# Another order for the opening of a one-core kernel: two loads on a second queue, zeroed decay rows, and an earlier read of the state sums

## The chip, the cores and the metric

The kernel runs on one core of one Trainium2 chip. The time is the device time of one execution, in microseconds; seven executions of the kernel before are given by their median. A profile of one execution gives the span (from the first to the last instruction of the program), every instruction with its engine and duration, and every DMA issue. The engines are TensorE (PE, with its weight loads PEld), VectorE (DVE), ScalarE (ACT), GpSimd (POOL) and SyncE (SP); SP and ACT also issue DMAs, and those entries are written SPq and ACTq.

## The reference

A recurrent attention with decay (batch 4, 8 heads, 768 tokens, head size 64), whose output is fed to a two-layer network with a leaky ReLU:

```python
gamma = 1.0 - 2.0 ** (-5.0 - np.arange(H))
for t in range(S):
    state = gamma[None, :, None, None] * state + einsum('bhd,bhe->bhde', k[:, :, t], v[:, :, t])
    y[:, :, t] = einsum('bhd,bhde->bhe', q[:, :, t], state) / sqrt(D)
x = y.transpose(0, 2, 1, 3).reshape(B * S, H * D)      # 3072 x 512
h = x @ w_in                                           # 512 x 2048
out = np.maximum(0.01 * h, h) @ w_out                  # 2048 x 512
```

The weights are float64 in memory; the rest is float32.

## The kernel before

The tokens are worked in six chunks of 128 (c = 0 to 5), each for four batches (b = 0 to 3). For one chunk and batch, `score` multiplies keys by queries into PSUM (L165), `masked` multiplies that by a triangular mask on VectorE into SBUF (L187), `decay_v` scales the values by a decay table (L147, or L151 on ScalarE), `reads` multiplies the state of earlier chunks by the queries (L201), `values` multiplies the masked scores by the values (L210), and `taken` scales the sum on VectorE and writes it to the token block x (L255). `state` sums keys times values (L225), and `state_taken` adds this to the state and decays it (L260, L261). For chunks 2 to 5 the score and the state sums have PSUM banks of their own (`score_apart`, L294, and `states_apart`), and `visit_with_scores` runs the attention of two batches between two stages of the network.

The network multiplies each block of 512 tokens by eight units of weights. A product of 2 x 2 blocks is made with seven block products instead of eight (`seven`, L521), from sums and differences of the blocks (L467, L470); `hidden` makes the first layer with the leaky ReLU (L556), `output` the second. Only the first unit of chunk 0 is multiplied plainly, in `direct` (tile d, L543): four steps for each half of the tokens, each step with one more piece of the weights, since the pieces come one after the other.

A piece of weights is 128 x 512 float64 words, loaded raw (L394) and made float32 in two parts. `powers` makes the powers of two out of the exponent bits with three ScalarE instructions (L440, L442, L443) and uses the piece's own float32 place as scratch. `mantissas` makes the rest on VectorE: the upper bits (L452), the lower bits added (L461), the product with the power (L463).

The order on each engine is the program's; nothing reorders it. The change lies in the opening, written out by hand at L688 to L790. All loads but one go through SP's queue in this order: queries and keys of batch 0, its values, those of batch 1, weight pieces 0 and 1, queries and keys of batch 2, its values, pieces 2 and 3, batch 3, the keys needed for the states, then chunk 1. ScalarE's queue carries one, eight rows of decay tables (L696), which land in a corner of the tile t and are spread to 128 partitions by three small products: the decay per head and the decay per chunk into `tables` (L742, L744), and the decay per token into `spread` (L748); copies bring these to the SBUF tile `dec` (L747 on VectorE, L750 on ScalarE).

`keep_busy(n)` (L730) issues n products of zeros, which keep TensorE at work while it has nothing to do: seven at the start, one between the values of batches 0 and 1, three after the score of batch 2. Their zeros are 128x256 words of t, set on VectorE (L725). The mask is set on VectorE (L713) and made triangular on POOL (L714).

The order on TensorE is then: seven idle products, score 0, tables, spread, score 1, values 0, one idle product, values 1, score 2, three idle products, and the first two steps of d. On VectorE: mask of score 0, the copy of the tables, the decay of values 0, mask of score 1, x of batch 0, upper bits of piece 0, x of batch 1, the rest of piece 0, piece 1, mask of score 2, piece 2. On ScalarE: the copy of `spread`, powers of pieces 0 and 1, decay of values 2, powers of pieces 2 and 3. On POOL: the decay of values 1.

Of the kernel before, what the change touches and what calls it, by code (L numbers as in the profile page):

```python
# [9 lines left out]
FP32 = mybir.dt.float32  # L10
U32 = mybir.dt.uint32
U16 = mybir.dt.uint16
I16 = mybir.dt.int16
BF16 = mybir.dt.bfloat16
I64 = mybir.dt.int64
AF = mybir.ActivationFunctionType
ALU = mybir.AluOpType
# [6 lines left out]
def kernel(  # L24
# [35 lines left out]
    nc = tc.nc  # L60
    NC = S // C
    DM = H * D
    HP = H // 2
    NU = DF // 512
    N = B * C // 2
    f64 = weights.dtype == I64
# [3 lines left out]
    work = ctx.enter_context(tc.tile_pool(name="work", bufs=1))  # L70
# [44 lines left out]
    heads = {}  # L115
# [11 lines left out]
            y = flat[:, half : 2 * half].rearrange("p (s h d) -> p s h d", s=2, h=H)  # L127
        heads[c, b] = x, y

    def load_qk(c, b):  # L130
        nc.sync.dma_start(out=heads[c, b][0], in_=qk[c, b])

    def load_v(c, b):
        nc.sync.dma_start(out=heads[c, b][1][:, 1], in_=kv[c, b][:, 1])

    def load_k(c, b):
        nc.sync.dma_start(out=heads[c, b][1][:, 0], in_=kv[c, b][:, 0])
# [6 lines left out]
    def decay_v(c, b, engine=nc.gpsimd):  # L144
        v = heads[c, b][1][:, 1]
        if engine is not nc.scalar:
            engine.tensor_tensor(out=v, in0=v, in1=gk.unsqueeze(2).to_broadcast([128, H, D]),  # L147
                                 op=ALU.mult)
        else:
            for h in range(H):  # L150
                engine.activation(v[:, h], v[:, h], AF.Identity, scale=gk[:, h : h + 1])  # L151
# [6 lines left out]
    def score(c, b):  # L158

        x = heads[c, b][0]  # L160
        ps = scores[c, b] = two_banks(f"ap_{c}_{b}")
        for a in range(HP):
            for u in range(2):
                for j in range(2):
                    nc.tensor.matmul(ps[ts(u, 64), j, a, :], lhsT=x[ts(j, 64), 1, a, ts(u, 64)],  # L165
                                     rhs=x[ts(j, 64), 0, a, :])
# [18 lines left out]
    def masked(c, b):  # L185
        am = new_am(c, b)
        nc.vector.tensor_tensor(  # L187
            out=am.rearrange("p j a t -> p (j a) t"),
            in0=scores[c, b].rearrange("p j a t -> p (j a) t"),
            in1=mask.unsqueeze(1).to_broadcast([128, H, C]), op=ALU.mult)  # L190
        scores[c, b] = am
# [54 lines left out]
    def taken(c, b, xb):  # L246

        tokens_taken(c, b, xb)
        state_taken(c, b, for_state(sums_at[c, b]))
# [5 lines left out]
        nc.vector.tensor_tensor(out=blocks, in0=ps[:, :, 0 : HP // 2, :], in1=gq, op=ALU.mult)  # L255

    def state_taken(c, b, sp):
        sums_at.pop((c, b))
        if 0 < c < NC - 1:
            nc.vector.tensor_tensor(out=st[b], in0=st[b], in1=sp, op=ALU.add)  # L260
            nc.vector.tensor_tensor(out=st[b], in0=st[b],  # L261
                                    in1=gc.unsqueeze(2).to_broadcast([128, HP, D]), op=ALU.mult)

# [65 lines left out]
    def visit_with_scores(c, b, following, complete=False):  # L329

        x = xs[c][0]
        early, late = ((following[0], following[1] + i) for i in range(2))
        score_apart(*early)
        for i in range(2):
            reads(c, b + i)
        masked_apart(*early, 0)
        masked_apart(*early, 1)
        score_apart(*late)  # L340
        for i in range(2):
            values(c, b + i)
        masked_apart(*late, 0)
        for i in range(2):
            tokens_taken(c, b + i, x)
        sp = states_apart(c, b)
        if complete:
            if xs[c][1] is None:
                xs[c][1] = new_t(c, f"t_{c}")
            t = xs[c][1]  # L350
            for k in range(2):
                minus(t[:, 0, k], x[:, 1, k], x[:, 0, k])
                minus(t[:, 1, k], x[:, 3, k], t[:, 0, k])
        masked_apart(*late, 1)
        if complete:
            minus(t[:, 2], x[:, 2], t[:, 1])
            last_difference(x)
        for i in range(2):
            state_taken(c, b + i, sp[:, i])
        for i in range(2):  # L360
            ahead(c + 1, b + i)
        for at in (early, late):
            load_kv(*at)
        for at in (early, late):
            decay_v(*at)
# [3 lines left out]
    raws = {}  # L369
# [5 lines left out]
    def piece(n):  # L375

        k, h, i = n // 4, n // 2 % 2, n % 2
        if k < N_UNITS - 1:
            return unit(k)[:, 2 * h : 2 * h + 2, i, :]
        new_pair(h)  # L380
        return units[k][h][:, :, i, :]
# [11 lines left out]
            raws[n] = place.bitcast(I64)  # L393
        nc.sync.dma_start(out=raws[n], in_=weights[n])  # L394

    def next_powers():
        n = done["powers"]
        done["powers"] += 1
        if n < N_PIECES and f64:
            powers(n)  # L400

    def next_mantissas(between=None):

        n = done["mantissas"]
        done["mantissas"] += 1
        if f64 and between is None:
            mantissas(n)
        elif f64:
            mantissas_upper(n)
            between()  # L410
            mantissas_rest(n)
        elif between is not None:
            between()
        if n != 3:
            load_piece(n + 4 if n < 3 else n + 3)
        if n == N_PIECES - 1:
            new_pair(2)
            for b in range(AHEAD):
                load(2, b)
        if n % 4 == 3 and n > 7:  # L420
            add_sums(n // 4)

    def round_piece():

        next_mantissas()
        next_powers()

    zs = {}

    def powers(n):  # L430

        top = raws[n].bitcast(U16).rearrange("p (h n four) -> p h n four", four=4, h=2)[:, :, :, 3]
        z = zs[n] = work.tile([128, 2, W // 2], I16, tag="z", bufs=3, name=f"z{n}")
        x = piece(n)


        nc.scalar.activation(x, top, AF.Prelu, alpha=float(BEND), scale=1.0 / 16,  # L440
                             bias=-7.5 / 16 - TOP)
        nc.scalar.activation(z, x, AF.Prelu, alpha=1.0 / BEND, bias=-float(BEND))  # L442
        nc.scalar.activation(z.bitcast(U16), z, AF.Relu, scale=128.0, bias=32768.0)  # L443

    def mantissas(n):

        mantissas_upper(n)
        mantissas_rest(n)

    def mantissas_upper(n):  # L450
        hi = raws[n].bitcast(U32).rearrange("p (h n two) -> p h n two", two=2, h=2)[:, :, :, 1]
        nc.vector.tensor_scalar(out=piece(n).bitcast(U32), in0=hi, scalar1=0x000FFFFF,  # L452
                                scalar2=0x00100000, op0=ALU.bitwise_and, op1=ALU.bitwise_or)

    def mantissas_rest(n):
        z = zs.pop(n)
        words = raws.pop(n).bitcast(U32).rearrange("p (h n two) -> p h n two", two=2, h=2)
        lo = words[:, :, :, 0]
        f = piece(n)
        m = f.bitcast(U32)  # L460
        nc.vector.scalar_tensor_tensor(out=f, in0=lo, scalar=2.0 ** -32, in1=m,  # L461
                                       op0=ALU.mult, op1=ALU.add)
        nc.vector.scalar_tensor_tensor(out=f, in0=f, scalar=2.0 ** -20, in1=z.bitcast(BF16),  # L463
                                       op0=ALU.mult, op1=ALU.mult)

    def plus(out, a, b):
        nc.vector.tensor_tensor(out=out, in0=a, in1=b, op=ALU.add)  # L467
# [1 line left out]
    def minus(out, a, b):  # L469
        nc.vector.tensor_tensor(out=out, in0=a, in1=b, op=ALU.subtract)  # L470
# [21 lines left out]
    def last_difference(x):  # L492
        minus(x[:, 1], x[:, 3], x[:, 1])
# [198 lines left out]
    words = tile_x("words").rearrange("p i k n -> p (i k n)")[:, 0 : 2 * W]  # L692
    xs = {0: new_x(0)}
    x, t = xs[0]
    rows = t[0:H, 1:3].rearrange("p i k n -> p (i k n)")[:, 0 : decay.shape[1]]
    nc.scalar.dma_start(out=rows, in_=decay)  # L696
    load_qk(0, 0)
    load_v(0, 0)
    load_qk(0, 1)
    load_v(0, 1)  # L700
    load_piece(0)
    load_piece(1)
    load_qk(0, 2)
# [17 lines left out]

    nothing = t[:, 0, 0, :].bitcast(BF16)
    nc.vector.memset(t[:, 0, 0, :], 0.0)  # L725
    idle = psum.tile([128, 2, N], FP32, tag="ff", bufs=4, name="idle")

    def keep_busy(n):
        for _ in range(n):
            nc.tensor.matmul(idle.rearrange("p i n -> p (i n)"), lhsT=nothing[:, 0:128],  # L730
                             rhs=nothing, start=True, stop=True, skip_group_check=True)

# [2 lines left out]
    n_gq = HP * C  # L737
    ends = [0, C, C + H, 2 * C + H, 2 * C + H + n_gq, 2 * C + H + n_gq + HP]
    by_head, ones, place, g_q, g_c = (rows[:, i:j] for i, j in zip(ends, ends[1:]))
    keep_busy(7)  # L740
    score(0, 0)
    nc.tensor.matmul(tables[:, 0, 0:H], lhsT=by_head, rhs=ones, start=True, stop=True,  # L742
                     skip_group_check=True)
    nc.tensor.matmul(tables[:, 0, H : H + HP], lhsT=place, rhs=g_c, start=False, stop=True,  # L744
                     skip_group_check=True)
    masked(0, 0)
    nc.vector.tensor_copy(out=dec[:, n_gq:], in_=tables[:, 0, 0 : H + HP])  # L747
    nc.tensor.matmul(spread.rearrange("p i n -> p (i n)"), lhsT=place, rhs=g_q, start=True,  # L748
                     stop=True, skip_group_check=True)
    nc.scalar.copy(out=dec[:, 0:n_gq], in_=spread.rearrange("p i n -> p (i n)"))  # L750
    decay_v(0, 0, nc.vector)
    score(0, 1)
    values(0, 0)
    masked(0, 1)
    decay_v(0, 1)
    keep_busy(1)
    next_powers()
    taken(0, 0, x)
    values(0, 1)
    next_mantissas(lambda: taken(0, 1, x))  # L760
    next_powers()
    score(0, 2)
    keep_busy(3)
    steps = direct(0, 0, x, parts[0][1], 0)
    next(steps)
    next_mantissas()
# [204 lines left out]
```

## Time and profile before

| | |
|---|---|
| median of seven executions | 666.54 us (665.59 to 669.92) |
| the profiled execution | 665.59 us |
| its span | 663.9 us, 10517 instructions |
| TensorE busy | 657.9 us (99%) |
| VectorE, ScalarE, POOL busy | 368.7, 176.1 and 18.9 us |
| read from and written to memory | 41.97 and 6.29 MB |

A line of the profile gives the kernel's line, the engine, the operation, the tiles (out<-in), and the partitions by elements. In the timeline a row begins with its start and its length in us from the span's start; "x16" counts the instructions put together in it, and the bracket tells how long the engine had been idle and what ended that. A matmul of float32 is counted as two instructions. In the chain of work that ended last, each piece follows what released it.

### The profile page before, as it was taken

How to read it: one execution, taken by the hardware profiler on the slowest of the kernel's cores; microseconds unless marked ns; L12 is line 12 of the kernel's file. 1: busy time of each engine (PE TensorE's matmuls, PEld its weight loads, DVE VectorE, ACT ScalarE, POOL GpSimd, SP SyncE). 2: the span in 40 equal slices, each digit the busy share in tenths (PEclk: the TensorE clock that was granted, in tenths of full speed). 3: DMA queues.
4: the chain of work that ended last, by engine and by line, in shares of the span. 5: the costliest groups of instructions: out<-in, count | busy, mean ns of one | idle time of the engine just before them, and what ended most of it. 6: DMA issues, size and time to landing. Idle time of an engine off the chain costs nothing.

```text
span 663.9 us, 10517 instructions
## 1 busy us (share of the span) xinstructions
PE 657.9 (99%) x4537; PEld 574.4 (87%) x4537; DVE 368.7 (56%) x588; ACT 176.1 (27%) x322; POOL 18.9 (3%) x22
## 2 busy tenths in 40 slices
PE   8999999999999999999999999999999999999998
PEld 5888888888888888888888889888888888888886
DVE  5789969889888674243436414527333343431342
ACT  5854555264261002202102211300220210221210
POOL 0000000000000020001001001001000100000000
PEclk9999999999999999999999999999999999999999
DMA  8920312312322550020022003004000001000001
GB/s 327 402 100 33 126 64 74 117 65 105 118 69 90 223 192 1 0 99 30 1 86 105 1 1 127 1 16 176 1 0 32 34 0 48 17 0 1 1 0 63
DMA packets 15757, 48.92 MB, mean 74 GB/s; under 512 B 1752, under 2 KB 2008, under 8 KB 15712
## 3 DMA queue, kind: packets, MB, share of 16 engines
q1 hardware_dynamic: 15696, 48.24, 20.1%
q8 instruction: 35, 0.57, 0.3%
q14 instruction: 10, 0.08, 0.0%
q10 hardware_dynamic: 16, 0.02, 0.0%
HBM read 41.97 MB, written 6.29 MB: 73 GB/s over the span
## 4 chain that ended last, share of the span: by engine, by line
PE 98%; DMA 1%; SPq 1%; issue 0%; DVE 0%
PE B_o L521 13%; PE A_o L521 13%; PE C_o L521 12%; PE A_h L521 12%; PE C_h L521 12%; PE B_h L521 12%; PE D_o L521 6%; PE D_h L521 6%; PE yp L210 3%; PE d L543 2%; PE ap L294 2%; PE ap L165 1%; PE yp L201 1%; DMA in<-in_qk_dram 1%; PE sp L225 1%; PE yp L225 0%
## 5 line engine op out<-in xcount | busy, mean ns | idle before, releaser
L521 PE MATMUL A_h<-x,w 128*128 128x256 f32 x368 | 87.7, 381 | 0.0
L521 PEld LDWEIGHTS A_h<-x,w 128*128 128x128 f32 x368 | 69.3, 190 | 9.7 <-issue 0.2
L521 PE MATMUL A_o<-g,w 128*128 128x256 f32 x288 | 68.1, 379 | 0.0
L467 DVE TENSOR_TENSOR m<-m,B_h 128x512 f32<-128x512 f32 x23 | 15.8, 686 | 92.8 <-PE B_h L521 92.8
L521 PEld LDWEIGHTS A_o<-g,w 128*128 128x128 f32 x288 | 54.6, 190 | 7.6 <-issue 0.2
L561 ACT COPY m<-A_h 128x512 f32<-128x512 f32 x23 | 13.5, 586 | 175.8 <-PE A_h L521 155.5
L556 ACT ACTIVATE g<-g 128x512 f32<-128x512 f32 x69 | 42.0, 630 | 66.0 <-DVE g L467 66.0
L467 DVE TENSOR_TENSOR m<-m,B_o 128x512 f32<-128x512 f32 x16 | 11.0, 685 | 64.3 <-PE B_o L521 64.3
L521 PE MATMUL D_h<-t,w 128*128 128x256 f32 x184 | 43.5, 379 | 0.0
L521 PE MATMUL C_h<-x,w 128*128 128x256 f32 x184 | 43.5, 379 | 0.0
L521 PE MATMUL B_h<-t,w 128*128 128x256 f32 x184 | 43.5, 379 | 0.0
L521 PE MATMUL C_h<-t,w 128*128 128x256 f32 x184 | 43.5, 379 | 0.0
L521 PE MATMUL B_h<-x,w 128*128 128x256 f32 x184 | 43.5, 379 | 0.0
L521 PEld LDWEIGHTS B_h<-t,w 128*128 128x128 f32 x184 | 35.0, 190 | 4.8
L521 PEld LDWEIGHTS D_h<-t,w 128*128 128x128 f32 x184 | 35.0, 190 | 4.8
L521 PEld LDWEIGHTS C_h<-x,w 128*128 128x128 f32 x184 | 35.0, 190 | 4.8
L521 PEld LDWEIGHTS C_h<-t,w 128*128 128x128 f32 x184 | 35.0, 190 | 4.8
L521 PEld LDWEIGHTS B_h<-x,w 128*128 128x128 f32 x184 | 35.0, 190 | 4.8
L470 DVE TENSOR_TENSOR gd<-g,gd 128x512 f32<-128x512 f32 x48 | 33.2, 692 | 1.7
L521 PE MATMUL B_o<-gd,w 128*128 128x256 f32 x144 | 34.0, 379 | 0.0
L521 PE MATMUL C_o<-gd,w 128*128 128x256 f32 x144 | 34.0, 379 | 0.0
L521 PE MATMUL D_o<-gd,w 128*128 128x256 f32 x144 | 34.0, 379 | 0.0
(125 smaller groups left out, 996.2 us busy)
## 6 DMA issues: line engine op xcount, KB each, us to landing
raw<-in_weights_dram SPq DMA_DIRECT2D x31, 512.0 KB, 4.0
kv<-in_kv_dram SPq DMA_DIRECT2D x17, 512.0 KB, 5.0
out_dram<-o SPq DMA_DIRECT2D x23, 256.0 KB, 2.3
qk<-in_qk_dram SPq DMA_DIRECT2D x11, 512.0 KB, 3.6
o<-in_qk_dram SPq DMA_DIRECT2D x8, 512.0 KB, 3.4
in<-in_qk_dram SPq DMA_DIRECT2D x5, 512.0 KB, 7.8
in<-in_kv_dram SPq DMA_DIRECT2D x3, 512.0 KB, 8.1
kv<-in_kv_dram SPq DMA_DIRECT2D x4, 256.0 KB, 6.8
```

Source lines behind the costliest of these rows:

```text
L165: nc.tensor.matmul(ps[ts(u, 64), j, a, :], lhsT=x[ts(j, 64), 1, a, ts(u, 64)], rhs=x[ts(j, 64), 0, a, :])
L201: nc.tensor.matmul(ps[ts(i, 64), j, m, :], lhsT=st[b][ts(j, 64), a, :], rhs=x[ts(j, 64), 0, a, :], start=(m == 0), stop=False, skip_group_ ...
L210: nc.tensor.matmul(ps[ts(i, 64), j, m, :], lhsT=y[:, 1, 2 * a + j, :], rhs=am[:, j, a, :], start=(c == 0 and m == 0), stop=True, skip_grou ...
L225: nc.tensor.matmul(sp[ts(j, 64), a, :], lhsT=y[:, 0, 2 * a + j, :], rhs=y[:, 1, 2 * a + j, :], start=start, stop=True, skip_group_check=True)
L294: nc.tensor.matmul(ps[j][ts(u, 64), a, :], lhsT=x[ts(j, 64), 1, a, ts(u, 64)], rhs=x[ts(j, 64), 0, a, :])
L467: nc.vector.tensor_tensor(out=out, in0=a, in1=b, op=ALU.add)
L470: nc.vector.tensor_tensor(out=out, in0=a, in1=b, op=ALU.subtract)
L521: nc.tensor.matmul(half, lhsT=block(w, sa)[:, k, ts(i, 128)], rhs=rhs[:, k, :], start=(first and (i == 0 or split) and n == 0 and k == 0), ...
L543: nc.tensor.matmul(banks[r][:, i, :], lhsT=block(2 * u, r + 2 * kh)[:, k, ts(i, 128)], rhs=x[:, 2 * kh + th, k, :], start=(step == 0 and i ...
L556: nc.scalar.activation(g[:, i], g[:, i], AF.Prelu, alpha=0.01)
L561: nc.scalar.copy(out=got["m1"], in_=ps)
```

## The change

Four things are done. First, batch 1's queries and keys are asked for on ScalarE's queue, ahead of everything else there, and its values on the same queue after the decay rows. Second, the decay rows lie on 128 partitions that were set to zero before (half by POOL, half by VectorE), so that the three small products run over 128 partitions instead of 8; their load waits for these zeros. Third, the order of the opening is another one: ten idle products at the start and one after the score of batch 2; both scores come before `spread`; the copy of `tables` is ScalarE's, and the decay of values 0 and of values 1 is POOL's; pieces 0 and 1 get scratch tiles for their powers; and the VectorE work on piece 0 is laid around the x of batches 0 and 1. Fourth, in `visit_with_scores` both additions of the state sums come before the last difference of x, and both decays after it.

```diff
-    def load_qk(c, b):
-        nc.sync.dma_start(out=heads[c, b][0], in_=qk[c, b])
+    def load_qk(c, b, queue=nc.sync):
+        queue.dma_start(out=heads[c, b][0], in_=qk[c, b])
...
     def state_taken(c, b, sp):
+        state_added(c, b, sp)
+        state_decayed(c, b)
...
@@ visit_with_scores
             minus(t[:, 2], x[:, 2], t[:, 1])
+        for i in range(2):
+            state_added(c, b + i, sp[:, i])
+        if complete:
             last_difference(x)
         for i in range(2):
-            state_taken(c, b + i, sp[:, i])
+            state_decayed(c, b + i)
...
-        x = piece(n)
+        x = piece(n) if scratch is None else scratch
...
@@ the opening
-    rows = t[0:H, 1:3].rearrange("p i k n -> p (i k n)")[:, 0 : decay.shape[1]]
-    nc.scalar.dma_start(out=rows, in_=decay)
+    rows = t[:, 1:3].rearrange("p i k n -> p (i k n)")[:, 0 : decay.shape[1]]
+    nothing = t[:, 0, 0, 0:64].bitcast(BF16)
+    half = decay.shape[1] // 2
     load_qk(0, 0)
+    load_qk(0, 1, nc.scalar)
+    nc.vector.memset(t[:, 0, 0, 0:64], 0.0)
+    nc.gpsimd.memset(rows[:, :half], 0.0)
+    nc.vector.memset(rows[:, half:], 0.0)
+    nc.scalar.dma_start(out=rows[0:H], in_=decay)
     load_v(0, 0)
-    load_qk(0, 1)
-    load_v(0, 1)
+    load_v(0, 1, nc.scalar)
     load_piece(0)
...
-    nothing = t[:, 0, 0, :].bitcast(BF16)
-    nc.vector.memset(t[:, 0, 0, :], 0.0)
...
-            nc.tensor.matmul(idle.rearrange("p i n -> p (i n)"), lhsT=nothing[:, 0:128],
-                             rhs=nothing, start=True, stop=True, skip_group_check=True)
+            nc.tensor.matmul(idle.rearrange("p i (two n) -> p (i two) n", two=2), lhsT=nothing,
+                             rhs=nothing.unsqueeze(1).to_broadcast([128, 4, 128]),
+                             start=True, stop=True, skip_group_check=True)
...
-    keep_busy(7)
+    keep_busy(10)
     score(0, 0)
...
     masked(0, 0)
-    nc.vector.tensor_copy(out=dec[:, n_gq:], in_=tables[:, 0, 0 : H + HP])
+    nc.scalar.copy(out=dec[:, n_gq:], in_=tables[:, 0, 0 : H + HP])
+    decay_v(0, 0)
+    score(0, 1)
+    decay_v(0, 1)
+    masked(0, 1)
     nc.tensor.matmul(spread.rearrange("p i n -> p (i n)"), lhsT=place, rhs=g_q, start=True,
                      stop=True, skip_group_check=True)
     nc.scalar.copy(out=dec[:, 0:n_gq], in_=spread.rearrange("p i n -> p (i n)"))
-    decay_v(0, 0, nc.vector)
-    score(0, 1)
     values(0, 0)
-    masked(0, 1)
-    decay_v(0, 1)
+    values(0, 1)
+    next_powers(scratch("m1", 0))
+    begin_mantissas(lambda: taken(0, 0, x))
+    taken(0, 1, x)
+    end_mantissas()
+    next_powers(scratch("u2", 1))
+    score(0, 2)
     keep_busy(1)
-    next_powers()
-    taken(0, 0, x)
-    values(0, 1)
-    next_mantissas(lambda: taken(0, 1, x))
-    next_powers()
-    score(0, 2)
-    keep_busy(3)
     steps = direct(0, 0, x, parts[0][1], 0)
```

`begin_mantissas` issues the upper bits, then what it is given, then the lower bits; `end_mantissas` the product with the power and the next load. Without an argument the two together are what `next_mantissas` was.

More of the change, by code (lines that the diff above doesn't have):

```diff
@@ L128, in place_for, with load_v @@
         heads[c, b] = x, y
-    def load_qk(c, b):
-        nc.sync.dma_start(out=heads[c, b][0], in_=qk[c, b])
-    def load_v(c, b):
-        nc.sync.dma_start(out=heads[c, b][1][:, 1], in_=kv[c, b][:, 1])
+    def load_qk(c, b, queue=nc.sync):
+        queue.dma_start(out=heads[c, b][0], in_=qk[c, b])
+    def load_v(c, b, queue=nc.sync):
+        queue.dma_start(out=heads[c, b][1][:, 1], in_=kv[c, b][:, 1])
     def load_k(c, b):
@@ L257, in state_taken, with state_added @@
     def state_taken(c, b, sp):
+        state_added(c, b, sp)
+        state_decayed(c, b)
+    def state_added(c, b, sp):
         sums_at.pop((c, b))
@@ L260, in state_taken, with state_decayed @@
             nc.vector.tensor_tensor(out=st[b], in0=st[b], in1=sp, op=ALU.add)
+    def state_decayed(c, b):
+        if 0 < c < NC - 1:
             nc.vector.tensor_tensor(out=st[b], in0=st[b],
@@ L394, in load_piece, with next_powers @@
         nc.sync.dma_start(out=raws[n], in_=weights[n])
-    def next_powers():
+    def next_powers(scratch=None):
         n = done["powers"]
@@ L399, in next_powers, with begin_mantissas, end_mantissas @@
         if n < N_PIECES and f64:
-            powers(n)
-    def next_mantissas(between=None):
+            powers(n, scratch)
+    def begin_mantissas(between=None):
+        mantissas_begun(done["mantissas"], between)
+    def end_mantissas():
         n = done["mantissas"]
         done["mantissas"] += 1
[L406 to L413, printed above, removed]
+        mantissas_ended(n)
         if n != 3:
@@ L421, in next_mantissas @@
             add_sums(n // 4)
+    def next_mantissas():
+        begin_mantissas()
+        end_mantissas()
     def round_piece():
@@ L428, with powers @@
     zs = {}
-    def powers(n):
+    def powers(n, scratch):
         top = raws[n].bitcast(U16).rearrange("p (h n four) -> p h n four", four=4, h=2)[:, :, :, 3]
         z = zs[n] = work.tile([128, 2, W // 2], I16, tag="z", bufs=3, name=f"z{n}")
-        x = piece(n)
+        x = piece(n) if scratch is None else scratch
         nc.scalar.activation(x, top, AF.Prelu, alpha=float(BEND), scale=1.0 / 16,
@@ L443, in powers, with mantissas_begun, mantissas_ended @@
         nc.scalar.activation(z.bitcast(U16), z, AF.Relu, scale=128.0, bias=32768.0)
[L445 to L464, printed above, removed]
+    def mantissas_begun(n, between):
+        if f64:
+            words = raws[n].bitcast(U32).rearrange("p (h n two) -> p h n two", two=2, h=2)
+            f = piece(n)
+            m = f.bitcast(U32)
+            nc.vector.tensor_scalar(out=m, in0=words[:, :, :, 1], scalar1=0x000FFFFF,
+                                    scalar2=0x00100000, op0=ALU.bitwise_and, op1=ALU.bitwise_or)
+        if between is not None:
+            between()
+        if f64:
+            nc.vector.scalar_tensor_tensor(out=f, in0=words[:, :, :, 0], scalar=2.0 ** -32,
+                                           in1=m, op0=ALU.mult, op1=ALU.add)
+    def mantissas_ended(n):
+        if f64:
+            z, f = zs.pop(n), piece(n)
+            raws.pop(n)
+            nc.vector.scalar_tensor_tensor(out=f, in0=f, scalar=2.0 ** -20, in1=z.bitcast(BF16),
+                                           op0=ALU.mult, op1=ALU.mult)
     def plus(out, a, b):
@@ L739, with scratch @@
     by_head, ones, place, g_q, g_c = (rows[:, i:j] for i, j in zip(ends, ends[1:]))
-    keep_busy(7)
+    def scratch(name, n):
+        return work.tile([128, 2, N], FP32, tag=name, name=f"{name}_x{n}")
+    keep_busy(10)
     score(0, 0)
@@ L750 @@
     nc.scalar.copy(out=dec[:, 0:n_gq], in_=spread.rearrange("p i n -> p (i n)"))
-    decay_v(0, 0, nc.vector)
-    score(0, 1)
     values(0, 0)
-    masked(0, 1)
-    decay_v(0, 1)
-    keep_busy(1)
-    next_powers()
-    taken(0, 0, x)
-    values(0, 1)
-    next_mantissas(lambda: taken(0, 1, x))
-    next_powers()
-    score(0, 2)
-    keep_busy(3)
+    values(0, 1)
+    next_powers(scratch("m1", 0))
+    begin_mantissas(lambda: taken(0, 0, x))
+    taken(0, 1, x)
+    end_mantissas()
+    next_powers(scratch("u2", 1))
+    score(0, 2)
+    keep_busy(1)
     steps = direct(0, 0, x, parts[0][1], 0)
```

## The prediction

> **What bounds the kernel now.** The page first: the busy shares, then the chain that ended last.
>
> ```profile
> PE 657.9 (99%) x4537; PEld 574.4 (87%) x4537; DVE 368.7 (56%) x588; ACT 176.1 (27%) x322; POOL 18.9 (3%) x22
> ...
> PE 98%; DMA 1%; SPq 1%; issue 0%; DVE 0%
> ```
>
> TensorE is busy 99% and is 98% of the chain. So the span is TensorE's own work plus whatever keeps it from starting. Next the busy time by stretch, to see where the missing 1% lies (columns: PE, PEld, DVE, ACT, POOL busy, granted clock, DMA share, GB/s).
>
> ```profile
> 2.00:8.00 6.00, 5.63 (x49) 2.68 (x51) 1.78 (x3) 1.13 (x2) 0.00 (x0) 1.00 0.93 309
> 8.00:14.00 6.00, 4.94 (x100) 3.71 (x97) 4.78 (x9) 4.28 (x9) 1.04 (x1) 1.00 1.02 413
> 14.30:50.00 35.70, 35.70 (x530) 29.90 (x530) 28.84 (x43) 24.99 (x70) 0.00 (x0) 1.00 0.68 259
> 50.00:660.00 610.00, 610.00 (x3862) 537.30 (x3861) 332.12 (x533) 144.87 (x243) 17.33 (x16) 1.00 0.16 57
> ```
>
> From 14.3 us to 660 TensorE has no hole at all. Only the first 14 us are loose, and there the DMA engines are full (share 0.93 and 1.02) but move 309 GB/s at first and 413 later. Then the chain in order of time, its start:
>
> ```profile
> 4.54 7.76 DMA in<-in_qk_dram
> 12.30 0.14 issue
> 12.44 1.10 PE ap L165 x32
> 13.54 0.76 PE idle L730 x3
> 14.29 3.45 PE d L543 x16
> ```
>
> The wait that ends last is the landing of batch 2's queries and keys at 12.30. After it come the score of batch 2 and three idle matmuls (0.76, that is 0.25 each), and at 14.29 the first useful product (d, L543). "Start of d" is the number that the change can move: each us there is one us of span, as long as what follows arrives in time. Last, the timeline for what else d waits for:
>
> ```profile
> 1.70 1.38 SPq L131 DMA_DIRECT2D qk<-in_qk_dram  x1
> ...
> 9.75 0.68 ACT L440 ACTIVATE w<-raw 128x512 f32<-128x512 uint16 x1 [1.60 <-DMA raw<-in_weights_dram]
> ...
> 10.14 0.68 DVE L255 TENSOR_TENSOR x<-yp,dec 128x512 f32<-128x512 f32 x1
> ...
> 12.90 0.69 DVE L463 SCALAR_TENSOR_TENSOR w<-w,z 128x512 f32<-128x512 f32 x1
> ...
> 18.06 0.69 DVE L463 SCALAR_TENSOR_TENSOR w<-w,z 128x512 f32<-128x512 f32 x1
> ```
>
> SP needs 1.38 us to ask for batch 1's queries and keys, against 0.37 to 0.43 for its neighbours. Weight piece 0 is ready at 12.90 + 0.69 = 13.59, piece 2 at 18.75; the third step of d, which needs piece 2, starts at 19.73.
>
> **The change, part by part.**
>
> *Loads.* SP no longer issues batch 1's queries and keys (1.38) and values (0.43), so it asks for pieces 0 and 1 and batch 2 about 1.9 us sooner (1.38 + 0.43 + two gaps of 0.04). ScalarE issues the first at once, then waits for the two memsets, issues the decay rows and then the values. Behind that wait stand only the values of batch 1 and the table load (1.28, L750); their first user is far off, the copy of dec at about 7. The same 3.1 MB (six 512 KB or 256 KB loads and batch 2's own) must flow before batch 2 is complete. If the engines gain nothing, it lands at 12.30 as now. If all of 2 to 8 ran at 413 instead of 309 GB/s, 6 x 104 = 0.62 MB, or 1.5 us, would be won: 10.8. I take about a third, 11.8, since the low rate began before the long issue could matter.
>
> The Trainium skill, "DMA: Bandwidth & Descriptors", section "Issuing engines are not separate DMA queues", says that loads issued by several engines run on the same 16 DMA engines, interleaved, and save only the issuing time. By it alone the landing would stay near 12.30 and the change would be worth 0.5 us instead of 0.8; the rate of 309 against 413 GB/s is the row that leaves room for more.
>
> *Memsets.* The zeros for the idle matmuls shrink from 128x256 (0.27, L725) to 128x64 and come first: at most the 0.17 of 128x128 (L713). TensorE starts at about 1.1 instead of 1.39. The 128x390 halves are not in the trace: on VectorE 0.17 + 262 x 0.10/128 = 0.37 from the two rows; on POOL between 0.10 (128x1, L946) and 1.04 (its 128x512 product, L147), I take 0.8. Both are done by 2.0, and the decay rows, behind batch 1's 512 KB on one queue, should land by 6. At either end they are hidden, since the tables are first used at 6.5.
>
> *Ten idle matmuls for seven.* Their weight loads stand 0.43 apart, so TensorE is held till 1.1 + 4.3 = 5.4. The first score now starts at 4.62. It comes 0.8 later; but at 4.62 it ran at part speed (1.41 against 1.10 for the next), and at 5.4 it should run at full speed. And two loads now share the engines, so its operands land later than 4.5: between 4.5 and 5.7 (1 MB at 300 GB/s from 2.0, and a little). I take 5.5.
>
> *The new order on TensorE, from 5.5.* Score 0 1.03 (chain row): 6.5. Two small tables 0.47 (L742 to L748, 5.96 to 6.43), now with 128 rows: 7.0; the rows of weight loads 8x128 (0.15 each) and 128x128 (0.19 each) bound that difference to 0.04 a load, either way. Score 1 with its 0.2 switch: 8.2. Spread 0.85: 9.1. Values 0 and 1, 1.02 each: 10.1 and 11.1. Their covers: mask 0 6.7 to 7.9 and mask 1 8.4 to 9.6 (1.23 each); the table copy moves from VectorE (0.16) to ScalarE, 7.0 to 7.3; both decay products on POOL, 7.4 to 8.4 to 9.5 (1.04 each), where the first was 0.69 on VectorE. All are in time. If the POOL cover failed, values 0 would wait one for one.
>
> *VectorE up to piece 0.* It loses 0.16 + 0.69 and gets a finer order. The upper half of piece 0 (0.43) now has its own scratch and needs only the landing (9.7 at latest): 10.1. Then x 0 10.3 to 11.0, second step of piece 0 0.69: 11.7, x 1 0.69: 12.4, third step 0.69: 13.1. Its powers on ScalarE run 9.75 to 11.7 behind the spread copy, as now. So d cannot start before 13.2.
>
> *Fewer idle matmuls after score 2.* Two less: 0.5. If batch 2 still lands at 12.30, d starts at 12.44 + 1.10 + 0.25 = 13.8; with 11.8 at 13.3. **I take 13.3, which is 1.0 earlier.**
>
> *What is late next.* ScalarE's queue (powers 0, powers 1, decay of batch 2, powers 2) is full from 9.75 on in both, so piece 2 stays ready at 18.75. Its user wants to start at 19.73 - 1.0 = 18.73 and needs 0.15 after it: 18.9. So of 1.0 about 0.8 remains. Piece 1 is ready at 14.9 against 13.3 + 1.73 = 15.0: in time. Later loads (L131, L142, L394 from 14 on) keep one queue's rate and their users have 0.8 to 2 us of room.
>
> *States read sooner.* In the timeline around 241 to 249 the second sum of states ends at 246.34 and D_h, which takes that bank, starts at 246.80 with no hole before it. The sum moves 0.68 forward: nothing to gain. The last difference moves 0.8 back; its reader comes at about 250, five products later. Nothing, either way, while that cover of some 4 us holds.
>
> Sum: -0.8 on the profiled execution's 665.59 us (span 663.9 and 1.7 around it), so 664.8. It was the shortest of the seven shown; the median is 666.54. With the same saving there I forecast **665.7**.
>
> **Rivals.**
>
> *A, the forecast*, 665.7; its own range 665.0 to 666.4. 45%.
>
> *B, the loads are hidden anyway*: the landing stays at 12.30 and only the two idle matmuls go, -0.5, and half of it is lost to ScalarE's queue: 666.2. For it: the DMA share of 0.93 says that the engines were hardly idle. Against: the rate. 15%.
>
> *C, the opening is repaired whole*: the loads run at full rate, pieces come early enough to use 1.1 us, and the surplus of the median run over the shortest (666.54 - 665.59 = 0.95), which can only come from the loose 14 us, goes as well: -2.1, 664.4. For it: TensorE is dense from 14.3 on, so no other place can vary. Against: ScalarE's queue and the 13.2 above. 22%.
>
> *D, slower: sharing makes the first operands late.* Batch 0's and batch 1's loads interleave, the decay rows queue behind batch 1's on ScalarE's queue, and TensorE takes score 0, tables and score 1 in that order, so one late landing stops all. The forecast chain has 14.29 - 13.2 = 1.1 us of room: it decides from a landing of batch 0 later than 6.6, or of the decay rows later than 8.1. Beyond, each us costs one; 1.5 to 2.5 us past it gives 668.0 to 669.0. For it: the first 512 KB already took till 4.5, and one issue has stalled for 1.38 us. Against: 1 MB at 309 GB/s is through by 5.7. 18%.
>
> The same chance covers a hole in TensorE's work that loses the clock; the trace holds 1.00 across the hole of 1.18 us before score 2. The Trainium skill, "TensorE: Matmul & The Clock Gate", part 1, has the clock halve after an idle window of about 3.4 us; by it a hole of 0.8 to 1.3 us, as the sums above leave, costs nothing.
>
> **How the numbers follow.** Predicted is A, 665.7. The range 664.0 to 668.0 takes in A, B, most of C and the near part of D; about 2 in 10 stay out. 0.3%, 2.0 us, is about what a measurement of this kernel can tell from no change. Faster by more: most of C and the edge of A, 0.22. Slower by more: the far part of D, 0.14. Within: 0.64.
>
> **What would show it.** Right: batch 2's landing near 11.8, score 0 at 5.4 to 5.7 in full speed, d at 13.3, the third step of d held by piece 2 near 18.9. Wrong: score 0 after 6.6 or tables after 8 (D); a landing at 12.3 (B); d before 13 (C); a granted clock below 1.00 after 6; any hole after 50, where I cost the change at nothing.

## The result and the profile after

The changed kernel takes 665.43 us (median of 19 executions, 665.16 to 665.94), the kernel before beside it 666.87 (49 executions, 665.59 to 670.18). The ratio is 0.9974, with a 95% interval of 0.9965 to 0.9983: faster, and inside the 0.3% that were called no change. The ranges tell more than the medians. The shortest executions differ by 0.43 us, the longest by 4.24. The profiled execution took 665.71 us with a span of 663.6; the one of before took 665.59 with 663.9. So the profile of before is of one of its shortest executions, that of the kernel after of one of its longer ones (their spans go from 663.0 to 663.8). One of the 35 executions of the kernel before that ran beside e1 to e4 took 768.16 us at a mean granted clock of 0.85; it is left out below.

The page of the kernel after, its busy line, its chain by engine, and two stretches (columns as before):

```profile
PE 658.8 (99%) x4537; PEld 574.6 (87%) x4537; DVE 369.6 (56%) x587; ACT 176.2 (27%) x323; POOL 20.7 (3%) x24
PE 98%; DMA 1%; DVE 0%; issue 0%; DVEq 0%
```

```profile
2.00:8.00 6.00, 5.76 (x57) 2.99 (x59) 0.63 (x1) 1.45 (x2) 0.00 (x0) 1.00 0.95 357
8.00:14.00 6.00, 5.63 (x101) 3.97 (x90) 5.27 (x9) 4.00 (x7) 2.09 (x2) 1.00 1.03 409
```

The loads now move 357 GB/s in the first stretch instead of 309, and TensorE's holes from 8 to 14 us shrink from 1.06 to 0.37 us. The chain in order of time, its start:

```profile
0.80 4.89 DMA qk<-in_qk_dram
...
5.74 1.47 PE ap L165 x32
...
12.79 0.69 DVE w L474
13.53 3.85 PE d L554 x16
```

Batch 2 is gone from the chain: its queries and keys land at 11.21 (before: 12.30), and d waits for weight piece 0, which VectorE ends at 13.48. d starts at 13.53, by the chain 0.76 earlier. But its third step starts at 19.47 instead of 19.74 (19.73 for its weights), so 0.27 of the 0.76 is left, which is the 0.3 of the spans. The timeline shows what took the rest:

```profile
9.88 0.58 ACT L773 COPY dec<-spread 128x512 f32<-128x512 f32 x1 [1.92 <-PE spread L771]
10.36 0.70 ACT L450 ACTIVATE m_x<-raw 128x512 f32<-128x512 uint16 x1
...
14.64 0.69 DVE L474 SCALAR_TENSOR_TENSOR w<-w,z 128x512 f32<-128x512 f32 x1
...
15.38 1.59 PEld L554 LDWEIGHTS d<-x,w 128*128 128x128 f32 x8 [0.27 <-DVE w L474]
...
18.72 0.69 DVE L474 SCALAR_TENSOR_TENSOR w<-w,z 128x512 f32<-128x512 f32 x1
19.47 1.99 PE L554 MATMUL d<-x,w 128*128 128x256 f32 x8
```

The chain's rows tell where to look: d's first two steps take 3.85 us in the kernel after and 3.45 before. By the starts of single products the gain shrinks in steps.

| | before | after | gain |
|---|---|---|---|
| first product of d | 14.13 | 13.53 | 0.60 |
| second step of d | 15.86 | 15.38 | 0.47 |
| values of batch 2 | 17.68 | 17.31 | 0.37 |
| third step of d | 19.74 | 19.47 | 0.27 |

The chain's 14.29 for before is where the last idle product ends; d's first product had been issued at 14.13, so 0.16 of the 0.76 is only a way of counting. Before, d's two steps run through without a wait. After, the first waits for piece 0, the second for piece 1 (ready at 14.64 + 0.69 = 15.33, where the beat would be 13.53 + 1.73 = 15.26), the third for piece 2 (ready at 18.72 + 0.69 = 19.41). Behind a wait the second product follows the first after 0.32 us instead of 0.22, which is most of the first two losses. The third loss is the wait for piece 2: without it the third step would start 0.10 sooner, no more.

The powers of piece 0 start at 10.36 (before: 9.75), behind the copy of `spread`, and everything on ScalarE's queue after them is as much later; so piece 2 is ready at 19.41 instead of 18.75. The copy is late because `spread` is, and `spread` because score 0 is: it starts at 5.74 and takes 1.47 us, against 1.03 for score 1 at 7.75. Score 0 thus loses 0.44 us: the clock's record of this execution begins at 6.56, and half of the 0.82 until then is 0.41. The values of batch 0, x and piece 0 stand behind score 0 too.

The opening thus explains 0.3 us between these two executions. The median moved by 1.44. The experiments look for the rest.

### The profile page after: what moved, and what is told of

Same layout as the page of the kernel before. It is cut to its first block, busy times and chain, and to the rows that moved or that the text cites. A ratio compares the mean times of both kernels' runs of the same rounds, so it can differ in the third digit from the quotient of the medians.

```text
span 663.6 us, 10518 instructions
## 1 busy us (share of the span) xinstructions
PE 658.8 (99%) x4537; PEld 574.6 (87%) x4537; DVE 369.6 (56%) x587; ACT 176.2 (27%) x323; POOL 20.7 (3%) x24
## 3 DMA queue, kind: packets, MB, share of 16 engines
HBM read 41.97 MB, written 6.29 MB: 73 GB/s over the span
## 4 chain that ended last, share of the span: by engine, by line
PE 98%; DMA 1%; DVE 0%; issue 0%; DVEq 0%
PE B_o L532 13%; PE A_o L532 13%; PE C_o L532 12%; PE A_h L532 12%; PE C_h L532 12%; PE B_h L532 12%; PE D_o L532 6%; PE D_h L532 6%; PE yp L210 3%; PE d L554 2%; PE ap L301 2%; PE ap L165 2%; PE yp L201 1%; PE sp L225 1%; DMA qk<-in_qk_dram 1%; PE yp L225 0%
## 5 line engine op out<-in xcount | busy, mean ns | idle before, releaser
L147 POOL TENSOR_TENSOR kv<-kv,dec 128x512 f32<-128x512 f32 x18 | 19.8, 1098 | 496.0 <-DMA kv<-in_kv_dram 426.7
```

## The experiments

Three theories stood. *Loads*: the second queue brings the operands sooner. *Cover* (the clock theory of the expectations): ten idle products instead of seven close holes in the opening, and what is won is the long executions of the kernel before. *Sums* (later the port theory): the state sums read sooner remove a wait in the visits.

### Are the loads what counts?

**e1: the kernel after with one queue.** `load_qk(0, 1)` and `load_v(0, 1)` go back to SP, behind batch 0's values.

> The changed kernel with batch 1's two loads back on SP's queue, everything else as changed. Loads theory (the second queue brings batch 2's landing from 12.30 to 11.21 us and its steadiness): the landing goes back to 12.3 or later, the first d starts at 13.8 or later, the median rises to 666.3 or more and single executions reach 668 again. Clock theory (executions of the kernel before differ in when TensorE's full clock is granted, and the new order with ten idle products hides that): the median stays below 665.9 and no execution is above 666.5.

Measured: 665.67 us (665.32 to 665.92), ratio 0.9973 (0.9959 to 0.9987), span 663.5. The chain of this kernel:

```profile
1.06 4.45 PE idle L744 x10
5.50 1.54 PE ap L165 x32
```

With one queue batch 0 lands at 4.56 and waits for the idle products, batch 2 lands at 12.07, d starts at 13.63, and its third step at 19.40 (19.47 in the kernel after). All the same the time cannot be told from that of the kernel after. The theory of the loads falls: the second queue moves landings, and the end does not follow them.

**e2: the kernel before with two queues.** Both loads of batch 1 go to ScalarE's queue, the decay rows between them; nothing else is changed.

> The kernel before with only batch 1's two loads moved to ScalarE's queue (batch 1's queries and keys ahead of the decay rows, the values behind them). Loads theory: most of the gain is there, batch 2 lands near 11.2, the median falls to 665.8 or less and the long executions (668 to 670) are gone. Clock theory: the long executions stay, the highest is above 668, and the median stays above 666.2.

Measured: 670.88 us (667.91 to 671.57), ratio 1.0035 (1.0016 to 1.0053), span 669.2: slower. PE's timeline:

```profile
5.73 1.98 PE L165 MATMUL ap<-qk 64*64 64x128 f32 x32 [1.17 <-DMA qk<-in_qk_dram]
```

Batch 2 lands at 11.30 here, a whole 1.0 sooner than before, and the median is 3.8 us longer, which neither theory had expected. Sharing delays batch 0 to 5.7, seven idle products end 1.17 us before that, and TensorE then works at half speed (1.98 us for a score of 1.03, 2.05 for a spread of 1.05). The first full clock is recorded at 16.52. So the second queue needs the longer cover; by itself it costs.

### What is the cover worth?

**e3: the kernel before with `keep_busy(10)` for `keep_busy(7)`.**

> The kernel before with ten idle products at the start instead of seven, nothing else. Clock theory: without the hole before the first score the full clock comes at the latest one window after the start, the long executions are gone (none above 667.5) though the first score starts 1 us later. Loads theory: the spread stays, with executions above 668, and the median is 666.9 or a little more.

Measured: 666.82 us (665.96 to 667.49) against 667.11 beside it, ratio 0.9992 (0.9978 to 1.0005): the median is unclear. No long execution came, though: none of twelve is over 667.49, where seven of the other 34 of the kernel before beside them took 669.1 to 670.4. Twelve are few: at a rate of seven in 34, none in twelve comes up about once in sixteen times. But e1, e5, e6 and the kernel after have ten idle products too, and none of their 50 executions is over 666.62.

**e4: the kernel after with `keep_busy(7)` for `keep_busy(10)`.**

> The changed kernel with seven idle products at the start instead of ten. TensorE then has a hole of about 1.4 us before the first score (landing at 5.7). Clock theory: the grant of the full clock can be missed, some executions are above 667 and the median rises by 0.3 us or more. Loads theory: the first score waits for its landing at 5.69 anyway, the median stays within 0.3 us of 665.4 and nothing is above 666.5.

Measured: 668.24 us (665.34 to 669.22), ratio 1.0007 (0.9991 to 1.0023), span 664.7. The whole gain is gone, and the scatter is back. Two stretches of this kernel:

```profile
4.04:7.45 3.41, 2.12 (x49) 1.74 (x52) 0.83 (x1) 0.17 (x1) 0.00 (x0) 1.00 1.03 383
7.45:10.86 3.41, 3.41 (x32) 1.57 (x26) 2.10 (x3) 0.02 (x1) 2.09 (x2) 0.50 1.03 406
```

The stretches are cut where the granted clock changes. It is full from 4.04, halved from 7.45 to 10.87, full again: steps of 3.41 us. In the first stretch TensorE waits 1.18 us for batch 0 (5.37) and is busy for 2.12 of 3.41; in the next the clock is 0.50, and by the chains of the two kernels score 1 takes 1.63 us instead of 1.03 and `spread` 2.02 instead of 1.05. A hole of 1.2 us costs itself and, where a stretch at half clock follows, by estimate up to 1.7 us more (half of 3.41).

The record has the mean granted clock of every execution. This one reads 0.997: half of 3.41 us is 0.26% of the span. Of the kernel before, 14 of the 69 executions beside the experiments read 0.997 too; they took 666.96 to 668.16. None of e1, e3, e5, e6 and the kernel after reads below 0.999. So lost clock is part of the scatter of the kernel before itself. Its twelve executions above 669 us read 0.999 or 1.00, which doesn't tell that their clock was full: e2's profiled execution reads 0.999 at 671.07 us, and its stretch from 6.29 to 9.70 reads 1.00, although TensorE works at half speed there.

### Are the state sums worth anything?

**look1: the kernel before once more, for one profile.**

> The kernel before, unchanged, profiled once more. Clock theory: the grant of the full clock lies at another time than the 5.30 us of the first profile, and the span follows it: about 663.9 with a grant before 7 us, and 2 to 4 us longer if the grant comes after 9 us or is lost once. Loads theory: the span follows the landing of batch 2, whatever the grant.

Measured: 666.55 us, span 664.84, which is 0.97 above the first profile of the same code. About half is in the opening: batch 2 lands at 12.78 instead of 12.30, and d starts at 14.77 instead of 14.29. The first full clock is recorded at 6.78, and score 0 takes 1.99 us at half speed, but d waits for batch 2 all the same. The other half is far behind the opening, in the visit at 463, which no theory had in view. The timeline of this second profile:

```profile
462.51 1.04 POOL L147 TENSOR_TENSOR kv<-kv,dec 128x512 f32<-128x512 f32 x1 [51.32 <-DMA kv<-in_kv_dram]
462.69 1.15 DVE L261 TENSOR_TENSOR states<-states,dec 128x256 f32<-128x256 f32 x1
463.76 0.41 DVE L260 TENSOR_TENSOR states<-states,sp 128x256 f32<-128x256 f32 x1
...
464.31 1.97 PE L521 MATMUL D_h<-t,w 128*128 128x256 f32 x8 [0.26 <-DVE states L260]
```

POOL starts to scale values when their load lands. The state decay (L261) that starts just after takes 1.15 us where its median is 0.42. The second sum (L260) is queued behind it on VectorE, and D_h, which takes that sum's bank, starts 0.43 us later than the beat of the products before it. 0.48 + 0.43 = 0.91 is nearly all of the 0.97.

**e6: the kernel after with the state sums late**, each followed by its decay and both behind the last difference, as before.

> The changed kernel with the state sums added after the last difference again, as before. All theories expect nothing: the sum ends 0.24 us ahead of its user and the gap is hidden; the median stays within 0.15 us of 665.4. Should it rise by 0.3 us or more, the earlier read is worth something at one of the five places where the profile shows no wait.

Measured: 666.10 us (665.25 to 666.62), ratio 0.9977 (0.9966 to 0.9989), span 664.2. Three of eleven executions took 665.25 to 665.46, eight 665.96 to 666.62; none of the 19 of the kernel after is above 665.94. No theory had expected a rise. The opening is that of the kernel after (d at 13.49, its third step at 19.41). The visit at 245:

```profile
245.24 1.04 POOL L147 TENSOR_TENSOR kv<-kv,dec 128x512 f32<-128x512 f32 x1 [11.03 <-DMA kv<-in_kv_dram]
245.27 1.29 DVE L268 TENSOR_TENSOR states<-states,dec 128x256 f32<-128x256 f32 x1
...
247.04 1.32 PE L530 MATMUL D_h<-t,w 128*128 128x256 f32 x5 [0.40 <-DVE states L264]
```

The same sequence as in look1, in another visit: the second sum runs behind the lengthened decay (246.49 to 246.90), D_h starts 0.57 us late (C_h starts at 244.75 and takes 1.73 on the beat), and the span is 0.6 longer than that of the kernel after. The medians differ by 0.67, but come from two sets of runs whose ratios overlap. e5, which ran beside e6 and reads the sums early (it differs from the kernel after by its zeros), has all its eight executions between 665.11 and 665.48 and a median 0.86 below e6. So the size, 0.6 to 0.9, rests on this, on the two spans and on the shape of the executions, and the mechanism on the trace.

**e8: e6 with the values of the visits scaled on ScalarE instead of POOL.**

> The changed kernel with the state sums late again (as in the run whose median was 666.1), and with the decay of values in these visits on ScalarE instead of POOL. Port theory: with POOL silent the decays of the state take 0.42 us everywhere, D_h waits nowhere, and the median is back at 665.2 to 665.6. If the long decays came from the values' landing in memory at that moment, they stay, D_h still waits, and the median stays at 665.9 or more.

Measured: 674.66 us (673.81 to 676.35), ratio 1.0126 (1.0109 to 1.0143). The time says nothing of the sums, since ScalarE now waits for loads and holds up the copies of A_h (six holes of 0.8 to 1.8 us). But the disputed instruction is answered. Its line in this kernel (durations in ns, least, median and most), then in e6:

```profile
L268 DVE TENSOR_TENSOR states<-states,dec x16: 424/425/428, 36.2 to 469.1; 128x256 f32<-128x256 f32 x16
```

```profile
L268 DVE TENSOR_TENSOR states<-states,dec x16: 424/425/1293, 36.6 to 463.3; 128x256 f32<-128x256 f32 x16
```

Without a product on POOL none of the sixteen decays is lengthened, and D_h never waits for a sum. With it, some take three times as long. The kernel after has such decays too (up to 1294 ns), but both sums are over by then. The same holds in every profile: 47 of the 224 decays in the fourteen take 0.8 to 1.3 us, each of them starts while a product on POOL is running, and each ends 0.28 us after that product. (Three more start just behind the start of a product and keep their 0.41 to 0.42; there the product takes 1.3 us.) The ten sums that start beside such a product take 0.41 or 0.42.

**e7: the kernel before with only the sums first.**

> The kernel before with only the state sums added ahead of the last difference, the opening untouched. Port theory (in the kernel before, a decay of the state on VectorE that meets a decay of values on POOL takes 0.8 to 1.3 us instead of 0.42 and holds back the second sum, so that D_h waits up to 0.6 us, in some visits of some executions): the median falls by 0.4 to 0.7 us against the kernel before, but executions above 668 stay, since they come from the clock in the opening. If the opening alone made the gain: no change of the median.

Measured: 666.16 us (665.59 to 669.07) against 666.54 beside it, ratio 0.9994 (0.9979 to 1.0009): unclear. Its profile has no wait of D_h, but a clock lost at 8.43 in the opening, as in e4, and a long execution stays (one of eleven; three more read 0.997). The median fell by 0.38 where 0.4 to 0.7 was expected; under the scatter of seven idle products that is not told from nothing.

### Are the zeros and the 128 rows needed?

**e5: the kernel after without the zeros**, the small products over 8 partitions again, the load of the decay rows waiting for nothing.

> The changed kernel with the three small products over eight partitions again: no zeros, the decay rows' load waits for nothing. Clock theory in its narrow form (what must not happen is a hole in time): the median stays within 0.2 us of 665.4 and nothing is above 666.3. Clock theory in its wide form (products over eight partitions don't count as work for the clock, and their 1 to 2 us are as good as a hole): the clock is lost in some executions, the median rises by 0.5 us or more and some are above 667. Loads theory: the same or 0.1 us less, as the rows come sooner.

Measured: 665.24 us (665.11 to 665.48), ratio 0.9973 (0.9962 to 0.9983), span 663.3. In the chain of this kernel score 0 starts at 5.80 and takes 1.10 instead of 1.47, since this execution's clock is full from 4.17; d starts at 13.22 and its third step at 19.14. That could be the phase of the clock or the missing zeros. e8 tells: its opening is that of the kernel after, zeros and all, and in its profile the clock is full from 4.67. Its chain:

```profile
5.54 1.10 PE ap L165 x32
...
13.19 3.86 PE d L552 x16
```

There the third step of d starts at 19.03. So an early full clock is enough for such a start. In three profiles in which it comes at 6.51 to 6.56 (e1, e6, the kernel after), the third step starts at 19.40 to 19.47. In eight executions the zeros were worth nothing; the version is the fastest here, by 0.19 us in the median, which these intervals do not resolve.

### Three attempts to start sooner

**v1: the decay rows ahead of batch 1 on ScalarE's queue**, nine idle products, the values of batch 2 scaled on POOL.

> A version meant to be faster than both: the changed kernel with the decay rows ahead of batch 1's two loads on ScalarE's queue, nine idle products instead of ten, and the decay of batch 2's values on POOL instead of ScalarE. If batch 0 lands at 4.7 instead of 5.7 for want of a second load beside it, score 0 starts at 5.1 instead of 5.7, the first d at 12.9 to 13.1, and piece 2, no longer behind ScalarE's 2.0 us of decay, waits for nobody: 0.6 to 1.0 us less, a median of 664.5 to 664.9. If batch 0 lands late all the same, TensorE has a hole of 0.6 us behind nine idle products: by the clock theory some executions are then above 666.5.

Measured: 669.69 us (668.95 to 670.01), ratio 1.0036 (1.0023 to 1.0048). The chain of this kernel, two lines:

```profile
2.12 7.41 DMA qk<-in_qk_dram
...
9.57 1.55 PE ap L165 x32
```

Batch 1, asked for at 2.12 instead of 0.80, lands at 9.53 instead of 5.89. TensorE waits 2.14 us for it and loses the clock from 10.08 to 13.49. d starts at 17.01.

**v2 and v3: e5 with batches 0 and 1 split in halves by partition over both queues**, nine idle products (v2) or eight (v3).

> A version meant to beat both: the changed kernel with eight decay rows (as in the run whose median was 665.24), with batch 0's and then batch 1's queries and keys cut in halves of 64 partitions over both queues, and nine idle products. Loads: batch 0 no longer shares the engines with batch 1 and should land at 4.2 to 4.7, batch 1 near 5.8; score 0 then starts at 5.0 when the idle products end, d at 12.9, the third step of d at 18.9: 664.8 to 665.0. Clock theory: no hole before or after score 0, so nothing above 665.6. If batch 0 lands at 5.7 all the same, a hole of 0.7 us opens and some executions are above 666.5.

> The same with eight idle products. Score 0 then starts at its landing or at 4.5, whichever is later: another 0.2 to 0.4 us less, 664.5 to 664.8, if the landing is before 4.6. With a later landing the hole before score 0 costs the clock in some executions, as with seven idle products: some above 666.5 and a median above that of nine.

Measured: 669.49 us (668.38 to 670.77), ratio 1.0046 (1.0033 to 1.0059), and 670.52 (669.10 to 671.03), ratio 1.0059 (1.0045 to 1.0073). The chain of v2:

```profile
2.30 6.60 DMA t<-decay_dram
8.90 0.04 issue
```

The decay rows, behind two halves on ScalarE's queue, land at 8.90 (v3: 8.50). Score 0 is early, the tables wait, and the clock goes in the stretch in which TensorE is busy for 1.79 of 3.41 us:

```profile
6.90:10.31 3.41, 1.79 (x49) 1.53 (x42) 1.22 (x1) 0.17 (x1) 0.47 (x1) 1.00 1.03 346
```

This is rival D's mechanism, at its place: rows later than 8.1 and a hole. Its price is not D's. D took one us for each us, so 0.8 us past 8.1 (v3: 0.4) would have cost that much; it said 668 to 669 for 1.5 to 2.5 us. The clock at half, to 17.14 in v2 and 16.88 in v3, cost the rest. All three attempts missed what was expected of them.

## Why the prediction was right, and where it was not

The forecast was 665.7 and 0.64 for no change; 665.43 came. That the number is so near is partly luck. The forecast was 0.84 below its median of before, 666.54; the median fell by 1.44, from 666.87. The -0.8 was to come from an earlier d alone, and of that 0.3 was there in the profiled execution. The sums and the long executions, which gave the rest, were put at nothing. Point by point:

- **What bounds the kernel: right.** TensorE is 98% of the chain in both, and the wait for batch 2 was the last one before d. But d's start of 14.29 was the end of an idle product; its first product starts at 14.13.
- **Loads: the landing was right and worth little.** I took 11.8 between 10.8 and 12.3; it is 11.21. Piece 0 then sets d, at 13.53 against the 13.2 to 13.3 of the sum. But e1 has no second queue and the same time.
- **Score 0 at full speed from 5.5: wrong.** It starts at 5.74 and takes 1.47 instead of 1.03. This is the mis-sized term: 0.2 late and 0.4 at half clock, it passes on to d and, through `spread` and the copy, to ScalarE's queue. (`spread` was put at 0.85 and takes 1.05, score 1 at 1.2 and takes 1.03; these two cancel.) Where score 0 does run at full speed, in e8, the sum nearly holds: d at 13.19, its third step 0.71 earlier than before.
- **What is late next: half right.** Piece 2 was named, ready at 18.75 as before. It is ready at 19.41, since the powers of piece 0 start 0.6 later, and it does hold the third step, for 0.10. Piece 1 was put at 14.9 and in time; it is ready at 15.33 and holds the second step. By the chain's count the loss is 0.5, not 0.2; by single products it is 0.33.
- **States read sooner, "nothing to gain": wrong.** I looked at one visit of one execution, in which the sum ended 0.46 before D_h. In look1 and e6 a decay that runs beside POOL's product pushes the sum past D_h, for 0.43 and 0.57 us. The Trainium skill, "SBUF — State Buffer", section "Who interferes with whom", describes a port pair shared by VectorE and GpSimd that only one holds at a time, and says that a VectorE instruction with two SBUF inputs contends with a GpSimd instruction that reads SBUF. The runs agree: the decay (two SBUF inputs) goes from 424 to as much as 1294 ns, the sum (one input from PSUM) takes 0.41 beside POOL too.
- **"No other place can vary": wrong for the same reason.** Of the 0.97 between the two profiles of before, 0.43 came from a visit at 463 us.
- **A hole of 0.8 to 1.3 us costs nothing by the page's window of about 3.4 us: wrong in e4.** The clock does move in steps of 3.41 us, as the Trainium skill, "TensorE: Matmul & The Clock Gate", part 1, has it. But a full idle window was not needed: stretches busy for 2.12 (e4), 1.79 (v2) and 1.27 us (v1) of 3.41 lost it. The row that the prediction read as a hole of 1.18 us at a clock of 1.00 was the weight loads' idle time; TensorE's own hole there is 0.97. What saved the forecast is that the kernel after has no such hole.
- **Rival C's idea was part of the truth:** the surplus of the median over the shortest execution went (0.27 us is left of 1.28). Its sum of -2.1 was too large.

The gain of 1.44 in the median, by parts, as an estimate: 0.3 to 0.7 from the opening (third step of d at 19.47 in the profile after and 19.03 in e8's, against 19.74), about 0.6 from the sums (e6), and the rest from the end of the long executions. That ten idle products end them is shown by e4, and by five of the kernels with ten (e1, e3, e5, e6 and the kernel after), none of which has one; the sixth, e8, is slow for its holes. That executions of the kernel before lose their clock for a stretch is on record (14 of 69, at 0.997). That the ones above 669 us got theirs late is argued from e2; no profile of that kernel itself fell on one. The parts do not simply add: with seven idle products the new order is worth nothing (e4), and with ten the old order gains 0.3 us by its median, which is not told from nothing (e3). Between e3 and e1, which ran beside each other and both have ten, lie 1.15 us; there the new order and the sums are at work, without the second queue.

Still open: whether the zeros matter in an execution with a lost clock, and what decides that the clock is lost. The busy share alone does not. Stretches with 0.60 (look1, 10.19 to 13.61) and 0.73 (e3, 8.95 to 12.36) kept it, while e4's 0.62 and e7's 0.82 (5.02 to 8.43) lost it.

## What to carry to other kernels

Cover the wait for the first operands with idle work that is a little too long rather than a little too short: three spare products cost nothing measurable here (e3), and three too few cost 2.2 us by the ratios and 2.8 by the medians (e4). Profile the kernel before twice: what differs between two profiles of one code is what a change can win without making anything shorter. Where an engine in order ends a buffer that another waits for, put that instruction ahead of those whose length depends on a third engine.

## What the runs showed of the hardware

- A load asked for 1.3 us later can land 3.6 us later: batch 1's 512 KB, asked for at 0.80, land at 5.89; asked for at 2.12, after weight piece 0 was asked for at 1.70, they land at 9.53 (v1). Small loads fare no better: the decay rows took 6.60 us in v2.
- Two loads of 512 KB asked for at once land at 5.69 and 5.89; with the second asked for 0.9 us later, the first lands at 4.56 (e1) or 4.57 (before).
- At half clock, a stretch of 3.41 us with TensorE full by the record did not bring the clock back where `spread` ran over 8 partitions (v2, 10.31 to 13.72; the next one did), while one did where it ran over 128 (e4, 7.45 to 10.86; v1, 10.08 to 13.49). That products over few partitions count for less would explain it, and would give the zeros a use; it is argued from a few profiles and was not tried by itself. e2 fits less simply: from 9.70 to 13.11 `spread` over 8 partitions fills only the first 0.9 us, TensorE is busy throughout, and the clock does not come.
